# Splitting a weight load unevenly over the two halves of the partitions, in a decode kernel with attention and an MLP

## The chip, the cores and the metric

The kernel runs on one core of a Trainium2 chip. The metric is the device time of one execution in microseconds (us), as the median of several runs. One further execution was taken with the hardware profiler; the profile that is quoted comes from it.

## The reference

One decode step for a batch of two tokens. The input is normalized once and goes both to an attention block over a long cache and to a two-layer MLP; both results are added to the input.

```python
def _A_ref(x, k_cache, v_cache, wq, wo):          # x: 2 x 1 x 512
    B, Sq, D = x.shape
    H, Dh = 32, 128                                # caches: 2 x 32 x 8192 x 128, bf16
    q = (x @ wq).reshape(B, Sq, H, Dh).transpose(0, 2, 1, 3)
    scores = jnp.einsum("bhqd,bhkd->bhqk", q, k_cache) * (Dh ** -0.5)
    p = _softmax(scores, axis=-1)
    o = jnp.einsum("bhqk,bhkd->bhqd", p, v_cache)
    return o.transpose(0, 2, 1, 3).reshape(B, Sq, H * Dh) @ wo

def _B_ref(x, w1, w2):                             # w1: 512 x 1792, w2: 1792 x 512
    h = jnp.maximum(jnp.einsum("bsd,df->bsf", x, w1), 0)
    return jnp.einsum("bsf,fd->bsd", h, w2)

xn = _layernorm(x)                                 # x = A_x; B_x is not used
return x + _A_ref(xn, K, V, wq, wo) + _B_ref(xn, w1, w2)
```

K and V together are 268 MB, the weights 12 MB. All arrays are bf16.

## The kernel before

The kernel writes its five instruction streams out by hand: SP issues loads, PE does matmuls and transposes, DVE (vector) and ACT (scalar) empty PSUM, POOL prepares constants and small copies. Semaphores tie them together; there is no scheduler that reorders anything.

**Loads.** All large loads go through SP's queue in the order in which they are written (L163 to L187): wq into the second V buffer, w1, w2, then K0, K1, V0. The 64 heads (2 tokens x 32) are taken two at a time, as 32 pairs; the K of a pair is one load of 4 MB (`load_k`, L158), and so is its V (`load_v`, L161): 128 partitions with 32 KB each. There are two K buffers and two V buffers. The next K load is issued when PE has done the last group of transposes of the pair that holds the buffer (`pT[NG - 1]`), the next V load when PE has finished the weighted sum of the pair that holds its buffer (`sW`). At the end the last V comes in two halves and wo in five pieces of 14, 7, 6, 3 and 2 rows a partition (`cuts`). The small load of x goes by ACT's queue (L164).

**The opening.** DVE and ACT compute the layer norm; PE transposes xn (L234) and multiplies it with wq (L240, 32 matmuls), then with w1 (L253, 56 matmuls), whose result `hp` lies transposed in PSUM: hidden unit f on a partition. Of w2 each partition p holds the 14 consecutive rows 14p to 14p+13 (L170), and w1's columns are read with a stride of 14 to match. DVE takes the relu of `hp` into `hT` (L446). PE waits for `hT` and for w2 (`dW2`) and runs 14 matmuls of 128 x 2 by 128 x 512 into `y` (L270). DVE adds x and leaves the sum in `ys` (L456). Only then does PE begin the loop over the pairs.

**The loop.** For a pair, PE transposes K in 16 groups of eight 128 x 128 blocks (L285), DVE and ACT copy each group to SBUF (L412), and PE multiplies it with q (L292). The weighted sum of V (L305) is that of the pair before, whose softmax is already done. The order on PE is fixed in `step`.

**The closing.** PE sums the softmax denominators (L360) and puts `ys` transposed into the PSUM tile `fin` with four fp32 matmuls against a 2 x 2 identity (L363), with `start` on the first; then the weighted sum of the last V, small transposes and selections (L378, L383), and the 128 matmuls with wo (L397), which accumulate onto `fin` piece by piece as `dW` allows. DVE casts `fin` to `yT` (L502), PE transposes it (L406), DVE copies it out (L504), and SP stores it (L189).

Of the kernel before, what the change touches and what calls it, by code (L numbers as in the profile page):

```python
# [7 lines left out]
ALU = mybir.AluOpType  # L8
# [11 lines left out]
def kernel(  # L20
# [13 lines left out]
    P = 128  # L34
    HP = P // 2
    bf16 = mybir.dt.bfloat16
    f32 = mybir.dt.float32

    Bsz, Sq, D = A_x.shape
    _, H, Sk, Dh = A_k_cache.shape  # L40
    Dff = B_w1.shape[1]
    assert Dh == P and D % P == 0 and Dff % P == 0 and Sk % HP == 0
    KT = D // P
    FT = Dff // P
# [3 lines left out]
    WJ = H * Dh // P  # L48
# [4 lines left out]
    QG = H * Dh // 512  # L53
    QH = 512 // Dh
    Z = (QG - 1) * Bsz
    inv_sqrt = float(Dh) ** -0.5
    eps = 1e-5

# [2 lines left out]
    def sb(shape, dt, name):  # L61
        return ctx.enter_context(nc.sbuf_tensor(name, shape, dt))
# [4 lines left out]
    def sem(name):  # L67
        return tc.alloc_semaphore(name)
# [2 lines left out]
    ks = [sb([P, SLOT], bf16, f"ks{i}") for i in range(R)]  # L71
    vs = [sb([P, SLOT], bf16, f"vs{i}") for i in range(R)]

    w_sb = sb([P, max(WJ * D, KT * Dff + FT * D)], bf16, "w_sb")
    w1_sb = w_sb[:, 0:KT * Dff].rearrange("p (kt f) -> p kt f", kt=KT)
    w2_sb = w_sb[:, KT * Dff:KT * Dff + FT * D].rearrange("p (j n) -> p j n", j=FT)
    wo_sb = w_sb[:, 0:WJ * D].rearrange("p (j n) -> p j n", j=WJ)
    kT = [sb([P, EG, P], bf16, f"kT{i}") for i in range(4)]
    identb = sb([P, P], bf16, "identb")
# [24 lines left out]
    OTn = sb([P, Bsz, H], bf16, "OTn")  # L104
    Ob = sb([H, Bsz, Dh], bf16, "Ob")
    OX = sb([P, WJ, Bsz], bf16, "OX")
    hT = sb([P, FT, Bsz], bf16, "hT")
    ys = sb([Bsz, D], f32, "ys")
    yT = sb([P, Bsz, KT], bf16, "yT")
    osb = sb([Bsz * KT, P], bf16, "osb")  # L110

# [11 lines left out]
        return Sc[i][:, 480:482]  # L123


    dX, dO, dW1, dW2 = sem("dX"), sem("dO"), sem("dW1"), sem("dW2")
    dK = [sem(f"dK{i}") for i in range(R)]
    dV = [sem(f"dV{i}") for i in range(R)]
    dH = [sem(f"dH{i}") for i in range(2)]
# [21 lines left out]
    )  # L151
    hp = ot[1][:, 0:FT * Bsz].rearrange("p (j b) -> p j b", b=Bsz)
    y = Sc[1][0:Bsz, :]
    fin = ot[0][:, 0:KT * Bsz].rearrange("p (b c) -> p c b", c=KT)


# [10 lines left out]
    @(lambda f: f(nc.sync))  # L167
    def _(sp):
        sp.dma_start(w1_sb, B_w1.rearrange("(p kt) f -> p kt f", kt=KT)).then_inc(dW1, 16)  # L169
        sp.dma_start(w2_sb, B_w2.rearrange("(p j) n -> p j n", j=FT)).then_inc(dW2, 16)  # L170
        load_k(0)
        load_k(1)
        load_v(0)
        for t in range(NP - 2):
            sp.wait_ge(pT[NG - 1], t + 1)
            load_k(t + R)
            sp.wait_ge(sW, t + 1)
            load_v(t + 1)
        sp.wait_ge(sW, NP - 1)
        for i in range(2):  # L180
            sl = slice(i * SLOT // 2, (i + 1) * SLOT // 2)
            sp.dma_start(  # L182
                vs[(NP - 1) % R][:, sl], V_all[(NP - 1) * P:NP * P, sl]
            ).then_inc(dH[i], 16)
        for c in range(NC):
            sl = slice(cuts[c], cuts[c + 1])
            sp.dma_start(wo_sb[:, sl, :], wo_v[:, sl, :]).then_inc(dW[c], 16)  # L187
        sp.wait_ge(sE, 1)
        sp.dma_start(  # L189
            out.rearrange("b s (c p) -> (b s c) p", p=P), osb[:]  # L190
        ).then_inc(dO, 16)
# [38 lines left out]
    def _(pe):  # L230
# [16 lines left out]
        i.then_inc(sQ, 1)  # L247
        pe.wait_ge(dW1, 16)

        w1_v = w1_sb.rearrange("p kt (f j) -> p kt j f", j=FT)  # L250
        for j in range(FT):
            for kt in range(KT):
                i = pe.matmul(  # L253
                    hp[:, j, :],
                    lhsT=w1_v[:, kt, j, :],
                    rhs=xz[:, kt, Z:Z + Bsz],
                    start=(kt == 0),
                    stop=(kt == KT - 1),
                )
# [6 lines left out]
        i.then_inc(sQ, 1)  # L266
        pe.wait_ge(sF, 2)
        pe.wait_ge(dW2, 16)
        for j in range(FT):
            i = pe.matmul(  # L270
                y,
                lhsT=hT[:, j, :],
                rhs=w2_sb[:, j, :],
                start=(j == 0),
                stop=(j == FT - 1),
            )
        i.then_inc(sF, 1)

# [81 lines left out]
            t = pe.matmul(dbp[:, :, u], lhsT=onesh[:, u, :], rhs=RS[:], start=True, stop=True)  # L360
        t.then_inc(sH, 1)
        for k in range(KT):
            pe.matmul(  # L363
                fin[:, k, :],
                lhsT=ys[:, k * P:(k + 1) * P],
                rhs=ident2[:],
                start=(k == 0),
                stop=False,
            )
        for i in range(2):  # L370
            pe.wait_ge(dH[i], 16)
            for e in range(i * NG // 2, (i + 1) * NG // 2):
# [9 lines left out]
        for dq in range(DQ):  # L382
# [4 lines left out]
                start=(dq == 0),  # L387
# [5 lines left out]
        for c in range(NC):  # L393
            pe.wait_ge(dW[c], 16)
            for j in range(cuts[c], cuts[c + 1]):
                for k in range(KT):
                    t = pe.matmul(  # L397
                        fin[:, k, :],
                        lhsT=wo_sb[:, j, k * P:(k + 1) * P],
                        rhs=OX[:, j, :],  # L400
                        start=False,
                        stop=(j == WJ - 1 and k == KT - 1),
                    )
        t.then_inc(sH, 1)
# [10 lines left out]
    @(lambda f: f(nc.vector))  # L415
    def _(v):
        v.memset(eps_t[:], eps).then_inc(sV, 1)
        v.memset(onesb[:], 1.0)
        v.memset(xz[:], 0.0).then_inc(sZ, 1)
        v.memset(prm[R - 1][:], 0.0).then_inc(sP, 1)  # L420
        v.wait_ge(dX, 16)
        v.bn_stats(out=stats[:], in_=xsb[:]).then_inc(sV, 1)
        v.wait_ge(sV, 2)
        v.bn_aggr(out=mv[:], in_=stats[:]).then_inc(sV, 1)
        v.wait_ge(sA, 1)
        v.reciprocal(out=rinv[:], in_=rstd[:]).then_inc(sV, 1)
        v.wait_ge(sV, 4)

        v.tensor_scalar(
            out=xn[:],  # L430
            in0=xsb[:].rearrange("b (p kt) -> b kt p", kt=KT),
            scalar1=mv[:, 0:1],
            scalar2=rinv[:, 0:1],
            op0=ALU.subtract,
            op1=ALU.mult,
        ).then_inc(sV, 1)
        v.wait_ge(sQ, 1)
        v.wait_ge(sZ, 1)
        v.tensor_copy(xz[:, :, Z:Z + Bsz], tpx).then_inc(sV, 1)
        v.wait_ge(sQ, 2)  # L440

        v.tensor_scalar(  # L442
            out=qs[:], in0=qp, scalar1=inv_sqrt, scalar2=None, op0=ALU.mult
        ).then_inc(sV, 1)
        v.wait_ge(sF, 1)
        v.tensor_scalar(  # L446
            out=hT[:], in0=hp, scalar1=0.0, scalar2=None, op0=ALU.max,
        ).then_inc(sF, 1)
        v.wait_ge(sQ, 3)

        v.tensor_copy(
            qb[:].rearrange("p (b g l) -> p l g b", b=Bsz, l=QH),
            tpq.rearrange("p l (g b) -> p l g b", b=Bsz),
        ).then_inc(sV, 93)
        v.wait_ge(sF, 3)
        v.tensor_tensor(out=ys[:], in0=y, in1=xsb[:], op=ALU.add).then_inc(sF, 1)  # L456

        def pair(i, n):
            for e in range(NG):
                if e not in ON_ACT:  # L460
                    v.wait_ge(pT[e], n)
                    kcopy(v, e)
            v.wait_ge(sS, n)
            for u in range(2):
                half = slice(u * HP, (u + 1) * HP)
                m = v.tensor_reduce(  # L466
                    out=mcol[i][half, :], in_=S_of(i)[half, :, u], axis=AX.X, op=ALU.max
                )
            m.then_inc(sM, 1)
            v.wait_ge(sT, n)  # L470
            v.tensor_reduce(  # L471
                out=mx[i][:], in_=tr_of(i).rearrange("o (u m) -> o u m", u=2),
                axis=AX.X, op=ALU.max, negate=True,
            ).then_inc(sX, 1)

        reg = nc.alloc_register(mybir.EngineType.DVE, "pairno_v")
        v.reg_mov(reg, 0)
        with v.Fori(0, NP // R):
            for r in range(R):
                v.reg_add(reg, reg, 1)  # L480
                pair(r, reg)

        v.wait_ge(sH, 1)
        v.reciprocal(out=RD[:], in_=Sc[0][:, 0:N]).then_inc(sV, 1)
        v.wait_ge(sV, 101)
        v.wait_ge(sO, NP + 1)
        on = OTn[:].rearrange("p b h -> p (b h)")
        v.tensor_tensor(
            out=on[:, 0:N - 2], in0=OTf[:, 2:N], in1=RD[:, 0:N - 2], op=ALU.mult
        ).then_inc(sV, 1)  # L490
        v.wait_ge(sW, NP + 1)
        v.tensor_tensor(
            out=on[:, N - 2:N], in0=ot[1][:, 0:2], in1=RD[:, N - 2:N], op=ALU.mult
        ).then_inc(sV, 1)
        v.wait_ge(sH, 2)
        v.tensor_copy(Ob[:], tp[0][0:H, 0:Bsz, :]).then_inc(sV, 1)
        v.wait_ge(sH, 3)
        v.tensor_copy(
            OX[:], Sc[1][:, 0:Bsz * WJ].rearrange("p (b j) -> p j b", b=Bsz)
        ).then_inc(sV, 1)  # L500
        v.wait_ge(sH, 4)
        v.tensor_copy(yT[:], ot[0][:, 0:KT * Bsz].rearrange("p (b c) -> p b c", c=KT)).then_inc(sV, 1)  # L502
        v.wait_ge(sH, 5)
        v.tensor_copy(osb[:], tp[1][0:Bsz * KT, 0, :]).then_inc(sE, 1)  # L504


    @(lambda f: f(nc.scalar))
    def _(a):
        a.wait_ge(sV, 3)
        a.activation(  # L510
            out=rstd[:], in_=mv[:, 1:2], func=ACTF.Sqrt, bias=eps_t[:Bsz], scale=1.0
        ).then_inc(sA, 1)


        def out_copy(r, n, c):
# [59 lines left out]
```

## Time and profile before

| | |
|---|---|
| median of 3 runs | 660.92 us (660.83 to 660.98) |
| profiled execution: time, span | 660.69 us, 658.6 us |
| busy share PE, weight loads, DVE, ACT, POOL | 85%, 81%, 38%, 39%, 1% |
| moved by DMA | 280.66 MB, 426 GB/s over the span |
| granted TensorE clock, mean | 0.944 |
| median from issue to landing, K load and V load | 26.7 us, 31.3 us |

A busy share is an average over the whole span; of several engines with high shares, the one that sets the time is found by asking what each waits for. PE's share includes modelled ends of pipelined matmuls. A queue's line in the profile gives packets (one for each row of a load and one for each engine's semaphore write), megabytes, and the time of its packets as a share of the sixteen DMA engines' span. In the timeline, a line gives start, duration, engine, line of the kernel and what is written and read; in brackets stands the idle time ahead of it and what ended it. The chain of work that ended last is put down to DMA for 58% and to PE for 37%.

### The profile page before, as it was taken

The numbers are of one execution on the slowest core, as the hardware profiler recorded it, in microseconds if no ns is written. First come the engines' busy times: TensorE is split into PE (matmuls) and PEld (weight loads), VectorE is DVE, ScalarE is ACT, GpSimd is POOL, SyncE is SP. The second block draws the span as 40 slices with busy tenths as digits, with TensorE's granted clock in tenths as the row PEclk, the third lists the DMA queues.
The fourth block names the chain that finished last, engine by engine and source line by source line (L and its number), as shares of the span: only waits on it lengthen the run. The fifth ranks groups of instructions, "written<-read, shape, count | busy, mean of one in ns | idle before, by whom it ended". The sixth has DMA issues, their size and how long they took to land.

```text
span 658.6 us, 26859 instructions
## 1 busy us (share of the span) xinstructions
PE 559.9 (85%) x12737; PEld 535.1 (81%) x12737; DVE 253.2 (38%) x436; ACT 255.8 (39%) x403; POOL 9.0 (1%) x46
## 2 busy tenths in 40 slices
PE   2998799987989878879887887997878997887896
PEld 0488798987879878879887887987878987887895
DVE  1144344442434433334443343443434443333441
ACT  1043444443433434334353434344333444333340
POOL 1000000000000000000000000000000000000000
PEclk9799999998998988999898899898989998898988
DMA  8999999999999999999999999999999999999996
GB/s 365 430 444 418 439 430 429 432 428 442 422 442 424 436 428 432 432 428 444 420 442 428 432 430 430 434 430 442 424 436 428 432 432 428 440 424 442 426 424 281
DMA packets 10542, 280.66 MB, mean 426 GB/s; under 512 B 1186, under 2 KB 1188, under 8 KB 1700
## 3 DMA queue, kind: packets, MB, share of 16 engines
q1 hardware_dynamic: 10528, 280.50, 99.2%
q8 instruction: 9, 0.15, 0.1%
q14 instruction: 1, 0.01, 0.0%
q10 hardware_dynamic: 4, 0.00, 0.0%
HBM read 280.50 MB, written 0.00 MB: 426 GB/s over the span
## 4 chain that ended last, share of the span: by engine, by line
DMA 58%; PE 37%; ACT 2%; issue 1%; SPq 1%; ACTq 0%; DVE 0%
DMA ks<-in_A_k_cache_dram 54%; PE tp L285 21%; PE Sc L292 11%; PE ot L305 4%; DMA w_sb<-in_A_wo_dram 4%; ACT kT L412 2%; ACT L412 1%; SPq L187 0%; PE Sc L340 0%; SPq L182 0%; PE Sc L343 0%; SPq L170 0%; SPq L169 0%; SPq L163 0%; PE ot L397 0%
## 5 line engine op out<-in xcount | busy, mean ns | idle before, releaser
L285 PE MATMUL tp<-identb,ks 128*128 128x128 bf16 x4096 | 323.5, 229 | 68.4 <-DMA ks<-in_A_k_cache_dram 68.4
L412 DVE COPY kT<-tp 128x1024 bf16<-128x1024 bf16 x320 | 219.7, 691 | 324.3 <-PE tp L285 324.2
L285 PEld LDWEIGHTS tp<-identb,ks 128*128 128x128 bf16 x4096 | 254.8, 102 | 72.3 <-DMA ks<-in_A_k_cache_dram 72.2
L412 ACT COPY kT<-tp 128x1024 bf16<-128x1024 bf16 x192 | 194.3, 1012 | 233.4 <-PE tp L285 233.3
L292 PE MATMUL Sc<-q,kT 128*128 128x64 bf16 x4096 | 216.8, 196 | 7.6 <-ACT kT L412 5.7
L292 PEld LDWEIGHTS Sc<-q,kT 128*128 128x128 bf16 x4096 | 178.4, 100 | 11.3 <-ACT kT L412 9.0
L305 PE MATMUL ot<-prm,vs 128*128 128x64 bf16 x4224 | 156.1, 192 | 4.2 <-issue 4.2
L305 PEld LDWEIGHTS ot<-prm,vs 128*128 128x128 bf16 x4224 | 139.0, 97 | 7.0 <-issue 4.4
L525 ACT COPY nm<-Sc 128x2 f32<-128x2 f32 x32 | 5.1, 160 | 118.5 <-PE Sc L343 118.5
L529 ACT ACTIVATE prm<-Sc,nm 64x128 bf16<-64x128 f32 x64 | 25.7, 401 | 4.3
L466 DVE TENSOR_REDUCE mcol<-Sc 64x1 bf16<-64x128 f32 x64 | 18.6, 290 | 18.7 <-PE Sc L292 18.3
L412 ACT ACT_TABLE_LOAD x16 | 20.5, 1283 | 2.2
L240 PE MATMUL ot<-vs,xz 128*16 128x512 bf16 x32 | 9.5, 470 | 8.6 <-DMA vs<-in_A_wq_dram 8.6
L517 ACT COPY OTf<-ot 128x2 f32 x32 | 5.1, 160 | 26.9 <-PE ot L305 26.9
L471 DVE TENSOR_REDUCE mx<-Sc 1x2 bf16<-1x128 bf16 x32 | 8.9, 278 | 16.9 <-PE Sc L340 16.9
L240 PEld LDWEIGHTS ot<-vs,xz 128*16 128x16 bf16 x32 | 3.3, 105 | 14.4 <-issue 12.2
L225 POOL COPY q<-qb 128x2 bf16<-128x2 bf16 x32 | 5.8, 184 | 588.9 <-PE Sc L292 566.1
L529 ACT ACTIVATION_READ_ACCUMULATOR prm<-Sc,nm x64 | 11.8, 185 | 0.0
L442 DVE TENSOR_SCALAR qs<-ot 16x512 bf16<-16x512 f32 x1 | 0.7, 679 | 18.0 <-PE ot L240 18.0
L340 PE MATMUL Sc<-identb,mcol 128*1 128x128 bf16 x32 | 7.0, 217 | 0.0
L270 PE MATMUL Sc<-w_sb,hT 128*2 128x512 bf16 x14 | 5.8, 604 | 0.1
L343 PE MATMUL Sc<-mx,onesb 1*128 1x2 bf16 x32 | 5.5, 172 | 0.0
(56 smaller groups left out, 37.5 us busy)
## 6 DMA issues: line engine op xcount, KB each, us to landing
ks<-in_A_k_cache_dram SPq DMA_DIRECT2D x32, 4096.0 KB, 26.7
vs<-in_A_v_cache_dram SPq DMA_DIRECT2D x31, 4096.0 KB, 31.3
vs<-in_A_wq_dram SPq DMA_DIRECT2D x1, 4096.0 KB, 12.1
vs<-in_A_v_cache_dram SPq DMA_DIRECT2D x2, 2048.0 KB, 19.3
w_sb<-in_B_w_dram SPq DMA_DIRECT2D x2, 1792.0 KB, 17.9
w_sb<-in_A_wo_dram SPq DMA_DIRECT2D x1, 1792.0 KB, 25.4
w_sb<-in_A_wo_dram SPq DMA_DIRECT2D x1, 896.0 KB, 27.1
w_sb<-in_A_wo_dram SPq DMA_DIRECT2D x1, 768.0 KB, 28.5
```

The lines of the kernel that those rows point to most:

```text
L225: g.tensor_copy(q2[t % R][:], qb[:, 2 * t:2 * t + 2]).then_inc(sQ1, 1)
L240: i = pe.matmul(qp, lhsT=xz[:, kt, Z - g * Bsz:Z - g * Bsz + QG * Bsz], rhs=vs[1][:, (kt * QG + g) * 512:(kt * QG + g + 1) * 512], start=( ...
L270: i = pe.matmul(y, lhsT=hT[:, j, :], rhs=w2_sb[:, j, :], start=(j == 0), stop=(j == FT - 1),)
L285: t = pe.transpose(tp[e % 4][:, i, :], ks[r][:, kk * Dh:(kk + 1) * Dh], identb[:])
L292: t = pe.matmul(Sc[r][:, 2 * kk:2 * kk + 2 * REP], lhsT=kT[e % 4][:, i, :], rhs=rep(q2[r][:]), start=True, stop=True,)
L305: t = pe.matmul(ot[r][:, 0:2 * REP], lhsT=vs[r][:, kk * Dh:(kk + 1) * Dh], rhs=rep(prm[r][:, kk, :]), start=(kk == 0), stop=(kk == KB - 1),)
L340: pe.transpose(tr_of(r), mcol[r][:], identb[:]).then_inc(sT, 1)
L343: pe.matmul(bc_of(r), lhsT=onesb[:], rhs=mx[r][:], start=True, stop=True).then_inc(sB, 1)
L412: fn(kT[e % 4][:], tp[e % 4][:]).then_inc(kR[e], 1)
L466: m = v.tensor_reduce(out=mcol[i][half, :], in_=S_of(i)[half, :, u], axis=AX.X, op=ALU.max)
L471: v.tensor_reduce(out=mx[i][:], in_=tr_of(i).rearrange("o (u m) -> o u m", u=2), axis=AX.X, op=ALU.max, negate=True,).then_inc(sX, 1)
L529: x = a.activation(out=prm[i][half, :, u], in_=S_of(i)[half, :, u], func=ACTF.Exp, bias=nm[i][half, u:u + 1], scale=1.0, accum_out=RS[half ...
```

## The change

The last 256 rows of w2 no longer lie on all 128 partitions. Every partition gets 12 consecutive rows of the first 1536 by SP's queue (`FA`), and the 256 rows that are left go to the lower 64 partitions alone, four to each (`FB`), so that the lower ones hold 16 and the upper ones 12. Those four rows come by ACT's queue, in eight loads of 8 partitions each: partitions p, p+4, ..., p+28, for p of 0 to 3 and 32 to 35, with four separate rows of 1 KB for each partition. They are issued by ACT after the square root of the layer norm and count on a semaphore of their own, `dW2b`.

What has to follow: w1's columns are read with a stride of 12 for the first 12 groups and without one for the last two; the relu becomes three instructions, of which two split the last two groups of `hp` into lower and upper halves and put both on the lower 64 partitions; PE waits for `dW2b` too, and runs 16 matmuls instead of 14, the last four on 64 partitions. The tile `w_sb` keeps its size, which wo sets.

Beside this, the closing takes `ys` in another way: PE transposes it into a corner of the PSUM bank of `fin`, DVE copies that to `xT`, the wo products start `fin` themselves, and the last cast becomes an addition of `xT`.

```diff
+    FA = FT - 2
+    FB = 2 * (FT - FA)
+    FJ = FA + FB
...
-    w2_sb = w_sb[:, KT * Dff:KT * Dff + FT * D].rearrange("p (j n) -> p j n", j=FT)
+    w2_sb = w_sb[:, KT * Dff:KT * Dff + FJ * D].rearrange("p (j n) -> p j n", j=FJ)
...
-        sp.dma_start(w2_sb, B_w2.rearrange("(p j) n -> p j n", j=FT)).then_inc(dW2, 16)
+        sp.dma_start(
+            w2_sb[:, 0:FA, :], B_w2[0:P * FA, :].rearrange("(p j) n -> p j n", j=FA)
+        ).then_inc(dW2, 16)
...
-        w1_v = w1_sb.rearrange("p kt (f j) -> p kt j f", j=FT)
+        w1_a = w1_sb[:, :, 0:P * FA].rearrange("p kt (f j) -> p kt j f", j=FA)
...
-                    lhsT=w1_v[:, kt, j, :],
+                    lhsT=w1_a[:, kt, j, :] if j < FA else w1_sb[:, kt, j * P:(j + 1) * P],
...
         pe.wait_ge(dW2, 16)
-        for j in range(FT):
+        pe.wait_ge(dW2b, 16 * 8)
+        for j in range(FJ):
+            half = slice(0, HP if j >= FA else P)
             i = pe.matmul(
                 y,
-                lhsT=hT[:, j, :],
-                rhs=w2_sb[:, j, :],
+                lhsT=hT[half, j, :],
+                rhs=w2_sb[half, j, :],
...
         for k in range(KT):
-            pe.matmul(
-                fin[:, k, :],
-                lhsT=ys[:, k * P:(k + 1) * P],
-                rhs=ident2[:],
-                start=(k == 0),
-                stop=False,
-            )
+            t = pe.transpose(yst[:, k, :], ys[:, k * P:(k + 1) * P], ident2[:])
+        t.then_inc(sH, 1)
...
-                        start=False,
+                        start=(j == 0 and k == 0),
...
-        v.tensor_scalar(
-            out=hT[:], in0=hp, scalar1=0.0, scalar2=None, op0=ALU.max,
-        ).then_inc(sF, 1)
+        for o, h in (
+            (hT[:, 0:FA, :], hp[:, 0:FA, :]),
+            (hT[0:HP, FA:FJ:2, :], hp[0:HP, FA:FT, :]),
+            (hT[0:HP, FA + 1:FJ:2, :], hp[HP:P, FA:FT, :]),
+        ):
+            t = v.tensor_scalar(out=o, in0=h, scalar1=0.0, scalar2=None, op0=ALU.max)
+        t.then_inc(sF, 1)
...
+        v.wait_ge(sH, 2)
+        v.tensor_copy(xT[:], yst)
...
-        v.tensor_copy(yT[:], ot[0][:, 0:KT * Bsz].rearrange("p (b c) -> p b c", c=KT)).then_inc(sV, 1)
+        v.tensor_tensor(
+            out=yT[:],
+            in0=ot[0][:, 0:KT * Bsz].rearrange("p (b c) -> p b c", c=KT),
+            in1=xT[:].rearrange("p c b -> p b c"),
+            op=ALU.add,
+        ).then_inc(sV, 1)
...
+        w2_v = B_w2[P * FA:, :].rearrange("(j p) n -> p j n", p=HP)
+        for p in (0, 1, 2, 3, 32, 33, 34, 35):
+            sl = slice(p, p + 29, 4)
+            a.dma_start(w2_sb[sl, FA:FJ, :], w2_v[sl]).then_inc(dW2b, 16)
```

More of the change, by code (lines that the diff above doesn't have):

```diff
@@ L72 @@
     vs = [sb([P, SLOT], bf16, f"vs{i}") for i in range(R)]
-    w_sb = sb([P, max(WJ * D, KT * Dff + FT * D)], bf16, "w_sb")
+    w_sb = sb([P, max(WJ * D, KT * Dff + FJ * D)], bf16, "w_sb")
     w1_sb = w_sb[:, 0:KT * Dff].rearrange("p (kt f) -> p kt f", kt=KT)
-    w2_sb = w_sb[:, KT * Dff:KT * Dff + FT * D].rearrange("p (j n) -> p j n", j=FT)
+    w2_sb = w_sb[:, KT * Dff:KT * Dff + FJ * D].rearrange("p (j n) -> p j n", j=FJ)
     wo_sb = w_sb[:, 0:WJ * D].rearrange("p (j n) -> p j n", j=WJ)
@@ L106 @@
     OX = sb([P, WJ, Bsz], bf16, "OX")
-    hT = sb([P, FT, Bsz], bf16, "hT")
+    hT = sb([P, FJ, Bsz], bf16, "hT")
     ys = sb([Bsz, D], f32, "ys")
+    xT = sb([P, KT, Bsz], f32, "xT")
     yT = sb([P, Bsz, KT], bf16, "yT")
@@ L123, in bc_of @@
         return Sc[i][:, 480:482]
-    dX, dO, dW1, dW2 = sem("dX"), sem("dO"), sem("dW1"), sem("dW2")
+    dX, dO, dW1 = sem("dX"), sem("dO"), sem("dW1")
+    dW2, dW2b = sem("dW2"), sem("dW2b")
     dK = [sem(f"dK{i}") for i in range(R)]
@@ L153 @@
     y = Sc[1][0:Bsz, :]
+    yst = ot[0][:, 16:16 + KT * Bsz].rearrange("p (c b) -> p c b", c=KT)
     fin = ot[0][:, 0:KT * Bsz].rearrange("p (b c) -> p c b", c=KT)
@@ L268, in _ @@
         pe.wait_ge(dW2, 16)
-        for j in range(FT):
+        pe.wait_ge(dW2b, 16 * 8)
+        for j in range(FJ):
+            half = slice(0, HP if j >= FA else P)
             i = pe.matmul(
                 y,
-                lhsT=hT[:, j, :],
-                rhs=w2_sb[:, j, :],
+                lhsT=hT[half, j, :],
+                rhs=w2_sb[half, j, :],
                 start=(j == 0),
-                stop=(j == FT - 1),
+                stop=(j == FJ - 1),
             )
@@ L494, in _ @@
         ).then_inc(sV, 1)
-        v.wait_ge(sH, 2)
+        v.wait_ge(sH, 3)
         v.tensor_copy(Ob[:], tp[0][0:H, 0:Bsz, :]).then_inc(sV, 1)
-        v.wait_ge(sH, 3)
+        v.wait_ge(sH, 4)
         v.tensor_copy(
@@ L500, in _ @@
         ).then_inc(sV, 1)
-        v.wait_ge(sH, 4)
-        v.tensor_copy(yT[:], ot[0][:, 0:KT * Bsz].rearrange("p (b c) -> p b c", c=KT)).then_inc(sV, 1)
         v.wait_ge(sH, 5)
+        v.tensor_tensor(
[4 more added lines that the diff above has]
+        ).then_inc(sV, 1)
+        v.wait_ge(sH, 6)
         v.tensor_copy(osb[:], tp[1][0:Bsz * KT, 0, :]).then_inc(sE, 1)
```

## The prediction

> **What bounds the kernel now.** I read the page first, then the waits of the DMA queue, then the timeline of the first 90 us and of the last 20, and last the trace's own records of packets and of semaphore landings, which give each DMA row's start and duration and, for each load, the sixteen times at which its engines finished.
>
> The page's list of DMA queues:
>
> ```profile
> DMA packets 10542, 280.66 MB, mean 426 GB/s; under 512 B 1186, under 2 KB 1188, under 8 KB 1700
> q1 hardware_dynamic: 10528, 280.50, 99.2%
> q8 instruction: 9, 0.15, 0.1%
> ```
>
> SP's queue (q1) fills the sixteen DMA engines for 99.2% of the span. So the time is the bytes of the slowest engine, so long as SP always has a load queued. Whether it has is seen in the waits of SP's queue (waited for: us in total, times, longest) and in its issues (start, us):
>
> ```profile
> SPq L158 <- PE tp L285: 429.8, 30, 39.8
> SPq L161 <- PE ot L305: 148.6, 30, 8.2
> ```
>
> ```profile
> 43.72 0.33 SPq L158 DMA_DIRECT2D ks<-in_A_k_cache_dram  x1
> ...
> 83.61 0.33 SPq L158 DMA_DIRECT2D ks<-in_A_k_cache_dram  x1
> ```
>
> Each K load waits for PE's transposes to free its buffer. The first load's rows start 1.04 us after its issue (0.96 to 2.00), so K2, issued at 43.72, could start at 44.8, while V0 ahead of it occupies its engines to 50.2 (landing 50.67 on most, and a row ends 0.43 before it is seen to land: 32.30 against 32.73 for K0). Spare: 5.5 us. For K4, issued at 83.61, V2 runs to 89.2: spare 4.5 us, the least of all. These spares decide below.
>
> PE's side, from the timeline:
>
> ```profile
> 26.50 5.84 PE L270 MATMUL Sc<-w_sb,hT 128*2 128x512 bf16 x14
> ...
> 32.77 1.51 PE L285 MATMUL tp<-identb,ks 128*128 128x128 bf16 x24 [0.43 <-DMA ks<-in_A_k_cache_dram]
> ...
> 654.90 0.37 PE L397 MATMUL ot<-OX,w_sb 128*128 128x2 bf16 x8 [0.16 <-DMA w_sb<-in_A_wo_dram]
> ```
>
> The w2 product (0.417 us a matmul) ends just before pair 0 begins. The end is set by the last wo piece: it lands at 654.85 and 3.7 us follow.
>
> The landing records show what the page doesn't: that last piece reached half of its engines at 653.04 to 653.44 and the other half at 654.67 to 654.85. The gap grew engine by engine: one engine falls 1.3 us behind at K0, seven are behind by 109 us, the eighth from 651. Each step follows one of the nine 16 KB instruction packets of q8 (29.6, 41.8, 47.8, 55.0, 61.1, 68.3, 107.2, 650.4, 654.3). Such a packet takes 1.06 us, fifteen data rows run beside it instead of sixteen, and the next row on its engine takes 1.7 us instead of 1.22. Eight late engines of sixteen: which? The x load of two rows ran just before wq; two engines land 0.1 us after their group from then on, and they are never among the late eight.
>
> [...]no view names engines, so the late half being the upper one is likely, not shown. [...]the fetch at 29.57 went between two rows of K0's load.[...]
>
> **The change part by part.**
>
> *Bytes.* The w2 load on SP's queue falls from 14,336 to 12,288 bytes a partition. A 14,336-byte packet took 0.5365 us; by the slope to 7,168 (0.2754) 12,288 costs 0.462. Eight on each engine: −0.6 us on all. [...]x's 1 KB took 0.044, 2 KB took 0.085, so 0.046 each, plus eight semaphore writes of 0.009: +1.54, net +0.94 us. Upper half: 654.85 − 0.6 = 654.25; lower: 653.44 + 0.94 = 654.38. The end would move by −0.47 us if nothing else happened.
>
> *ACT.* Eight issues after rstd (ends 3.49), at the 0.56 us of the x issue: to 8 us. ACT's next work for others is the copy of pair 0 at 33.4; the table load of 1.28 us between hides too. Cost nothing.
>
> *Matmuls and hT.* Two more w2 matmuls: 16 × 0.417 = 6.67 us, +0.83. The relu becomes three DVE instructions (0.19 once now; two small ones add about 0.3 with their gaps). Both delay pair 0 by about 1.1 us, less than the 4.5 us of spare: nothing by themselves. qb behind them comes 0.3 later, under the w2 product.
>
> *Tail.* Four transposes replace the four fp32 matmuls of L363 (1.05 us), with 8 columns' copy (about 0.17) on DVE; PE's V products follow at 644.6 and have slack to the wo pieces. From below: the matmuls' whole 1.05, hidden; from above the same again, hidden up to the 0.2 us by which PE waits for the 653.29 piece. The final add against the copy of 0.17: a tensor_tensor took 0.16 at 2 columns and 0.22 at 62, so +0 to 0.05 on the path.
>
> *The wait dW2b.* PE waits for all eight small loads ahead of its first w2 matmul; behind it stand pair 0's transposes, and behind these K2's issue. The rows first reach the engines at 3.49 + 0.95 (the x load's 0.92 to 1.87) = 4.4, when the third wq row (1.22 us each) is running. If ACT's queue gets one 1 KB row for each row of SP's, the 32 rows pair off with wq rows 3 to 8 (6), w1's 8, w2's 8, K0's 8 and two of K1's. K0 lands at 31.2 on an undisturbed engine; two rows (2.4) and the added 1.0 of bytes give 34.6. PE then starts pair 0 at 34.6 + 6.8 = 41.4 instead of 32.77: 8.6 us late. It catches up (pairs take it 16 to 17 us from the third on, a K and V load 19.4), but not in time: K2 and K4 come late, and the queue stands empty for 8.6 − 4.5 = 4.1 us by K4. That idle time levels the early lags, but the engine hit at 650.4 is still late at the end, so the balance brings nothing. The profiled execution took 660.69 (span 658.6): 664.8; the median is 0.2 higher, so **665.0**.
>
> How sure is 34.6? If semaphore writes also take turns, on both queues, 40 entries against nine a load end at K1's sixth row: 39.5, 13.5 us late, +9.0. If only SP's take turns, 31.0: +0.5 to 1. So this case spans 661.5 to 670.
>
> **The rivals.**
>
> *In time.* A load's four rows go as one packet, or ACT's rows are served faster than SP's: eight turns end inside wq, before 15 us, PE waits for nothing new, and only bytes count: −0.47 + 0.05, **660.5**. It ends on the other side; it decides from the point where the small loads land before about 30 us (start 4 us late, within the spare). For it: the 4.4 us arrival against a need at 27. Against: the fetch shows turns row by row for 32 KB rows. By this mechanism the gain can't exceed half the gap, 0.65 us, which is 0.1%.
>
> *A price for each turn.* The only change of queue in the trace is the instruction fetch: 1.33 us for 16 KB whose bytes are worth 0.62, so 0.71 is lost. If each of 32 turns costs that, 23 us more: the rows land at 57 and the end is 27 us later, **687**; with eight turns, 5.7 us on the lower half: 653.44 + 0.94 + 5.7, **666**. For it: the row after each fetch takes 0.46 longer. Against: [...]two filled queues may overlap.
>
> *The wrong half.* If the late engines were the lower ones, the bytes load them: +0.94, **661.9**.
>
> **How the numbers follow.** A measurement of this kernel tells about 0.2% (1.3 us) from no change. Turns row by row with PE waiting: 0.45 (0.40 slower, 0.05 within). In time: 0.30 (0.28 within, 0.02 faster). A price for each turn: 0.16, slower. The wrong half: 0.05, within. Something else: 0.04, half faster, half slower. Sum: faster 0.04, within 0.38, slower 0.58. The range, 660.2 to 671.5, holds the second case and nearly all of the first; most of the third is left out. The first case's own range is 661.5 to 670.
>
> **What would show it.** The 1 KB packets of ACT's queue spread from 4.4 to about 34 us (in time: all before 15; priced turns: each SP row between them 1.7 us). PE's wait ahead of the w2 matmuls put down to a w_sb load, ending at 31 to 40. Pair 0's transposes at 41. An empty stretch in the DMA rates near 50 us. In time instead: pair 0 at about 34, no new wait, and the last piece's sixteen landings within 0.5 us. The forecast is wrong if pair 0 starts before 37 or the DMA share stays at 99%.

## The result: 671.22 us, slower by 1.5%

The changed kernel takes 671.22 us in the median of six runs (669.76 to 671.87), the kernel before 660.95 (660.64 to 661.28). The ratio is 1.0153, 95% interval 1.014 to 1.0166. The profiled execution took 671.38 us with a span of 669.3, 10.7 above the span of before.

The forecast was 665.0 with a range of 660.2 to 671.5: the way and the mechanism hold, but the change measured, 10.3 us, is two and a half times the 4.1 that were forecast.

The page's list of DMA queues, changed kernel:

```profile
DMA packets 10863, 280.67 MB, mean 419 GB/s; under 512 B 1250, under 2 KB 1508, under 8 KB 2020
...
q1 hardware_dynamic: 10528, 280.24, 97.6%
q10 hardware_dynamic: 324, 0.26, 0.1%
```

SP's queue no longer fills the engines: 97.6% of the span against 99.2%. ACT's queue (q10) holds 324 packets: 256 rows of 1 KB and 64 semaphore writes from the small loads, and four packets from the x load. Where SP's queue stands empty is seen in the busy share of the DMA engines, in tenths, for forty equal slices of the span (the kernel before, then the changed one):

```profile
DMA  8999999999999999999999999999999999999996
...
DMA  8994999999999999999999999999999999999996
```

and closer in the busy time by stage (stage, its length, busy time of each engine, granted clock, DMA share, GB/s):

```profile
core 0: us, PE busy (x) PEld busy (x) DVE busy (x) ACT busy (x) POOL busy (x), PEclk, DMA share, GB/s
0.00:48.00 48.00, 19.65 (x113) 8.57 (x114) 3.65 (x14) 3.05 (x4) 3.44 (x16) 0.79 0.97 409
48.00:60.00 12.00, 11.79 (x275) 11.62 (x275) 7.50 (x11) 6.07 (x6) 0.00 (x0) 1.00 0.25 93
60.00:667.00 607.00, 527.84 (x12355) 514.16 (x12351) 242.38 (x414) 246.85 (x393) 5.60 (x30) 0.94 1.00 428
```

Between 48 and 60 us the DMA share is 0.25; before and after it is whole. The quarter is nearly all the end of V0; 9 us are lost in one place, while PE is at its busiest. The timeline shows who is late:

```profile
3.21 5.82 ACTq L535 DMA_DIRECT2D w_sb<-in_B_w_dram  x8
...
41.94 6.09 PE L281 MATMUL Sc<-w_sb,hT 128*2 128x512 bf16 x16 [15.09 <-DMA w_sb<-in_B_w_dram]
47.97 1.51 PE L296 MATMUL tp<-identb,ks 128*128 128x128 bf16 x24
...
58.91 0.33 SPq L165 DMA_DIRECT2D ks<-in_A_k_cache_dram  x1
```

PE waits 15.09 us for a load into w_sb, begins pair 0 at 47.97 instead of 32.77 (15.2 us late), and K2 is issued 15.2 us late, at 58.91 instead of 43.72. V0, the last load in the queue, had left its engines between 49.7 and 51.2.

The packet records show the small rows themselves. They don't name engines, but an engine's packets follow each other end to start and can be chained. Each small load writes its semaphore on eight engines (64 writes for eight loads), by the chains on the same eight each time. The forecast calls these eight the lower ones and the other eight the upper, and so does what follows; which partitions an engine writes no view shows. On each of the eight engines that carry small rows, one entry of ACT's queue (a 1 KB row of 0.046 us, or a semaphore write of 0.009) follows one entry of SP's queue; this pair is called a turn below. So the four rows of a partition are four turns, which the prediction had left open. The first rows run at 7.66 us, and the eight loads end, counted by their semaphore writes, at about 12.7, 15.0, 17.3, 19.8, 22.5, 28.8, 33.8 and 40.1 (two engines one turn later, at 41.1 and 41.3). The last landing is at 41.81.

### The profile page after: what moved, and what is told of

It reads as the page before. It is cut to its first block, busy times and chain, and to the rows that moved or that the text cites. A ratio compares the mean times of both kernels' runs of the same rounds, so it can differ in the third digit from the quotient of the medians.

```text
span 669.3 us, 26866 instructions
## 1 busy us (share of the span) xinstructions
PE 559.3 (84%) x12735; PEld 534.4 (80%) x12735; DVE 253.5 (38%) x439; ACT 256.0 (38%) x403; POOL 9.0 (1%) x46
## 3 DMA queue, kind: packets, MB, share of 16 engines
q1 hardware_dynamic: 10528, 280.24, 97.6%
## 4 chain that ended last, share of the span: by engine, by line
DMA 58%; PE 37%; ACT 2%; issue 1%; ACTq 1%; SPq 0%; DVE 0%
DMA ks<-in_A_k_cache_dram 48%; PE tp L296 21%; PE Sc L303 11%; DMA w_sb<-in_B_w_dram 5%; DMA w_sb<-in_A_wo_dram 4%; PE ot L316 4%; ACT kT L418 2%; PE Sc L281 1%; ACTq L535 1%; ACT L418 1%; SPq L196 0%; DMA xsb<-in_A_x_dram 0%; PE Sc L351 0%; SPq L191 0%; PE Sc L354 0%
## 5 line engine op out<-in xcount | busy, mean ns | idle before, releaser
L281 PE MATMUL Sc<-w_sb,hT 128*2 128x512 bf16 (+1 forms) x16 | 6.1, 557 | 15.1 <-DMA w_sb<-in_B_w_dram 15.1
L281 PEld LDWEIGHTS Sc<-w_sb,hT 128*2 128x2 bf16 (+1 forms) x16 | 1.6, 110 | 19.1 <-issue 18.9
```

The lines of the kernel that those rows point to most:

```text
L281: i = pe.matmul(y, lhsT=hT[half, j, :], rhs=w2_sb[half, j, :], start=(j == 0), stop=(j == FJ - 1),)
```

## The experiments

Seven kernels, told in the order of what they settle. "Theory" in the quoted expectations is what was held before each ran.

**Same rows, no turns.** The eight small loads go by SP's queue, behind its w2 load.

```diff
         ).then_inc(dW2, 16)
+        w2_v = B_w2[P * FA:, :].rearrange("(j p) n -> p j n", p=HP)
+        for p in (0, 1, 2, 3, 32, 33, 34, 35):
+            sl = slice(p, p + 29, 4)
+            sp.dma_start(w2_sb[sl, FA:FJ, :], w2_v[sl]).then_inc(dW2b, 16)
         load_k(0)
...
-            a.dma_start(w2_sb[sl, FA:FJ, :], w2_v[sl]).then_inc(dW2b, 16)
```

> The changed kernel with the eight small w2 loads issued by SP right behind its w2 load, instead of by ACT. Nothing takes turns. Theory (the loss is the late landing of rows that take turns one by one on ACT's queue): the small rows land at about 22.5, PE does not wait for them, pair 0 starts at about 34.5, the DMA share is back at 99%, and only the bytes count: 660.4 to 660.6 us, with the last wo piece landing on all sixteen engines within 0.5 us, because the late half is the upper one. Rival (the split itself, the 64-partition matmuls, the relu in three parts or the closing cost the time): 668 to 672. Rival (the late engines are the lower half): 661.9, with the last landings 2.8 us apart.

Measured: 661.55 us against 660.87, ratio 1.0011 (1.0003 to 1.002). The timeline:

```profile
2.35 5.85 SPq L183 DMA_DIRECT2D w_sb<-in_B_w_dram  x8
...
26.39 6.23 PE L285 MATMUL Sc<-w_sb,hT 128*2 128x512 bf16 x16 [0.31 <-DVE hT L461]
...
32.55 1.51 PE L300 MATMUL tp<-identb,ks 128*128 128x128 bf16 x24
```

The small rows land at 22.9, PE waits for hT alone, pair 0 starts at 32.55, and nearly all of the loss is gone. So the split, the 64-partition matmuls, the relu in three parts and the closing are not what costs 10 us. But the forecast gain of 0.3 to 0.5 us is not there either: the time is 0.7 us above the kernel before, and the last wo piece reaches the sixteen engines 3.0 us apart instead of within 0.5. By these two numbers the last rival (661.9 and 2.8 us apart) comes closer than the theory; the groups of landings further below show how far it holds.

**Same queue, fewer entries.** The four rows of a partition are consecutive, so each 8-row load has eight rows of 4 KB.

```diff
-        w2_v = B_w2[P * FA:, :].rearrange("(j p) n -> p j n", p=HP)
+        w2_v = B_w2[P * FA:, :].rearrange("(p j) n -> p j n", p=HP)
...
+        w1_b = w1_sb[:, :, P * FA:].rearrange("p kt (f j) -> p kt j f", j=FB)
-        for j in range(FT):
+        for j in range(FJ):
             for kt in range(KT):
                 i = pe.matmul(
-                    hp[:, j, :],
-                    lhsT=w1_a[:, kt, j, :] if j < FA else w1_sb[:, kt, j * P:(j + 1) * P],
+                    hp[0:HP if j >= FA else P, j, :],
+                    lhsT=w1_a[:, kt, j, :] if j < FA else w1_b[:, kt, j - FA, :],
...
-            (hT[0:HP, FA:FJ:2, :], hp[0:HP, FA:FT, :]),
-            (hT[0:HP, FA + 1:FJ:2, :], hp[HP:P, FA:FT, :]),
+            (hT[0:HP, FA:FJ, :], hp[0:HP, FA:FJ, :]),
```

> The changed kernel with the last 256 rows of w2 dealt out so that the four rows of a partition are consecutive: each of the eight loads on ACT's queue has one row of 4 KB for each partition instead of four of 1 KB (w1's last columns read with a stride of 4, four products of 64 columns instead of two of 128). Same bytes, same queue, same loads; entries per engine fall from 40 to 16. Theory (one entry a turn, semaphore writes counted): from 7.7 us on 5 turns in wq, 9 in w1, 2 in w2: all landed by 19, PE does not wait, 660.4 to 660.7 us. Rival (turns cost by bytes or by load, or ACT's queue is slow whatever the entries): still landing at 35 to 41, 666 to 671.

Measured: 661.28 us against 660.87, ratio 1.0005 (0.9997 to 1.0013).

```profile
3.63 5.36 ACTq L535 DMA_DIRECT2D w_sb<-in_B_w_dram  x8
...
27.11 5.39 PE L282 MATMUL Sc<-w_sb,hT 128*2 128x512 bf16 x16 [0.15 <-DVE hT L457]
```

ACT issues at nearly the same pace, the first row runs at 7.65, the bytes are the same; what differs on the queue is that they come in fewer and longer entries. All has landed by 19.73 instead of 41.81, and PE waits for hT alone. The wait is set by entries, one a turn, not by bytes and not by ACT's queue as such. The time itself was forecast at 660.4 to 660.7; again the gain is missing, though the 0.4 us above the kernel before lie within the interval.

**The wait without the change.** The kernel before, with one line ahead of its w2 product:

```diff
         pe.wait_ge(dW2, 16)
+        pe.wait_ge(dK[1], 16)
```

> The kernel before with one more wait: PE waits for K1's landing (42.45 us in the profile) ahead of its w2 product. No split, no load on ACT's queue. Theory: the product runs 42.5 to 48.3, pair 0 starts 15.6 us late, K2 and K4 are issued late, SP's queue stands empty, and the end moves by 15.6 less K4's spare of 4.5: +11.1, 672.0 us, with an empty stretch at 51 to 60. Rival (the small loads cost the DMA engines time by themselves): clearly less, 665 or under.

Measured: 670.69 us against 660.87, ratio 1.0147 (1.0132 to 1.0163). Timeline, and the DMA row of the slices:

```profile
42.67 5.04 PE L271 MATMUL Sc<-w_sb,hT 128*2 128x512 bf16 x14 [15.72 <-DMA ks<-in_A_k_cache_dram]
47.65 1.51 PE L286 MATMUL tp<-identb,ks 128*128 128x128 bf16 x24
```

```profile
DMA  8994999999999999999999999999999999999996
```

Pair 0 starts 14.9 us late, the same fourth slice of 16.7 us is more than half empty as in the changed kernel, and the time is the changed kernel's but for half a microsecond. The late start of PE alone is enough for the whole loss; taking turns costs the DMA engines nothing that shows. The forecast of 672.0 was 1.3 too high: the w2 product took 5.04 us, not 5.8, and the spare that it subtracts is not the one that counted (see the part on the spare below).

**A smaller dose.** The same with K0's landing.

```diff
         pe.wait_ge(dW2, 16)
+        pe.wait_ge(dK[0], 16)
```

> The kernel before with one more wait: PE waits for K0's landing (32.73 us) ahead of its w2 product: pair 0 starts at about 38.7, 6.0 us late. Theory (a late start costs only what exceeds the least spare of SP's queue, K4's 4.5 us): +1.4, 662.3 us. Rival (a late start is paid in full): 667. Rival (all of it is caught up): 660.9.

Measured: 662.08 us against 660.87, ratio 1.0019 (1.0008 to 1.0029); its runs lie apart, 661.1 to 663.54.

```profile
38.75 1.51 PE L286 MATMUL tp<-identb,ks 128*128 128x128 bf16 x24
...
49.69 0.33 SPq L158 DMA_DIRECT2D ks<-in_A_k_cache_dram  x1
...
70.31 0.33 SPq L158 DMA_DIRECT2D ks<-in_A_k_cache_dram  x1
```

Six microseconds late cost 1.2 in the median. Lateness is paid only above a spare, as forecast; of the rivals, payment in full is ruled out. That the number fits (662.3 forecast) is in part luck: the profile, which is of the slowest of the eight executions, shows the engines partly idle from 50 to 52 and from 70 to 74, ahead of K2 and of K3, and not ahead of K4, whose spare the forecast subtracted. Why K3 came late there, and why the executions differ by 2.4 us, stays open.

**An earlier issue.** The changed kernel, with ACT's eight issues moved ahead of its wait for the statistics.

```diff
+        w2_v = B_w2[P * FA:, :].rearrange("(j p) n -> p j n", p=HP)
+        for p in (0, 1, 2, 3, 32, 33, 34, 35):
+            sl = slice(p, p + 29, 4)
+            a.dma_start(w2_sb[sl, FA:FJ, :], w2_v[sl]).then_inc(dW2b, 16)
         a.wait_ge(sV, 3)
...
-            a.dma_start(w2_sb[sl, FA:FJ, :], w2_v[sl]).then_inc(dW2b, 16)
```

> The changed kernel with the eight small loads issued by ACT at once after the x load, ahead of the wait for the statistics (1.5 us instead of 3.2). Theory (40 entries, one a turn, against the rows of SP's queue): the issue is 1.7 us earlier, so one or two more wq rows are paired off and the last row comes one or two K1 rows sooner: landing at 38.5 to 40.5, 669.0 to 670.5 us. Rival (ACT's late first row, 7.66, is what makes it late): the first row at about 2.5 and all landed before 30: 661 to 662.

Measured: 669.29 us against 660.9, ratio 1.0122 (1.0107 to 1.0138).

```profile
1.52 5.81 ACTq L529 DMA_DIRECT2D w_sb<-in_B_w_dram  x8
...
39.73 6.56 PE L281 MATMUL Sc<-w_sb,hT 128*2 128x512 bf16 x16 [13.32 <-DMA w_sb<-in_B_w_dram]
```

The first small row runs at 6.46 instead of 7.66, one wq row earlier, and the last lands at 39.59, in the forecast range. PE's product starts 2.2 us earlier: one turn of 1.2 us is the earlier first row, and the other is that here no engine is a turn behind. The count of turns is the cause, the start only shifts it.

**The closing alone.** The kernel before with the transposes, the copy and the addition of the changed closing.

```diff
-            pe.matmul(
-                fin[:, k, :],
-                lhsT=ys[:, k * P:(k + 1) * P],
-                rhs=ident2[:],
-                start=(k == 0),
-                stop=False,
-            )
+            t = pe.transpose(yst[:, k, :], ys[:, k * P:(k + 1) * P], ident2[:])
+        t.then_inc(sH, 1)
...
-                        start=False,
+                        start=(j == 0 and k == 0),
...
+        v.wait_ge(sH, 2)
+        v.tensor_copy(xT[:], yst)
...
-        v.tensor_copy(yT[:], ot[0][:, 0:KT * Bsz].rearrange("p (b c) -> p b c", c=KT)).then_inc(sV, 1)
...
+        v.tensor_tensor(
+            out=yT[:],
+            in0=ot[0][:, 0:KT * Bsz].rearrange("p (b c) -> p b c", c=KT),
+            in1=xT[:].rearrange("p c b -> p b c"),
+            op=ALU.add,
+        ).then_inc(sV, 1)
```

> The kernel before with the closing of the changed one alone: ys transposed into PSUM, copied to xT, added at the last cast. No split of w2. Theory (costs nothing): 660.8 to 661.0 us. Rival (the closing is the reason why the two versions without the late wait, small loads on SP's queue and one 4 KB row, stand 0.4 to 0.7 us above the kernel before): 661.3 to 661.6.

Measured: 660.89 us against 660.9, ratio 0.9999 (0.9991 to 1.0008). It costs nothing; the 0.4 to 0.7 us of the two versions above come from elsewhere.

**Which engines are late.** Where the gain went is read from the last landings of the two versions without the late wait. The last wo piece reaches the sixteen engines in three groups. With the small loads on SP's queue: two engines at 652.71 and 652.86, twelve at 653.88 to 654.60, two at 655.65 and 655.70. With 4 KB rows: two at 652.42 and 652.64, twelve at 653.73 to 654.38, two at 655.30 and 655.41. By the split the upper eight, which carry no small rows, are about 1.5 us ahead of the lower eight, as K0's landings show with the small loads on SP's queue (seven engines at 30.41 to 30.88, the eighth, hit by then, among the nine at 31.93 to 32.30), and an instruction fetch puts an engine 1.3 us back (in the kernel before, K0 lands on fifteen engines at 31.01 to 31.39, and at 32.73 on the one hit by the fetch at 29.57). So the twelve are the six upper engines that were hit with the six lower ones that were not, the first two are upper engines not hit, the last two lower ones that were. Followed load by load, the hits of both versions fall in the same order: three upper (five upper engines are left in front at V0), two lower (two engines stand alone at the end at K2), three upper (two are left in front at the end). The last two, which now carry the extra rows, end 0.85 and 0.56 us after the 654.85 of before; the times rose by 0.68 and 0.41, and only the first rise is clear of no change by its interval.

To see the same in the kernel before, marks were put on its engines:

```diff
...
+        mark_v = A_wo.rearrange("(p j) n -> p (j n)", j=16)
+        sl = slice(0, 29, 4)
+        sp.dma_start(mark[sl, :], mark_v[sl, :]).then_inc(dM, 16)
+        for p in (1, 2, 3):
+            sl = slice(p, p + 13, 4)
+            sp.dma_start(mark[sl, :], mark_v[sl, :]).then_inc(dM, 16)
+        for p in (32, 33, 34):
+            sl = slice(p, p + 5, 4)
+            sp.dma_start(mark[sl, :], mark_v[sl, :]).then_inc(dM, 16)
         load_k(0)
...
+        sp.wait_ge(dM, 16 * 7)
         sp.wait_ge(sE, 1)
```

> The kernel before with seven more loads on SP's queue behind w2, of 16 KB rows into a tile that nothing reads: one load of 8 partitions, three of 4, three of 2. [...]The marks stay apart through the whole run, so each engine that an instruction fetch delays by 1.3 us is seen to leave its own group. Theory A (the late eight are the upper half): all eight steps are seen in the unmarked group of eight. Theory B, after the 4 KB version and the one on SP's queue (six of the late are upper, two are lower): six steps in the unmarked group, two in the marked ones[...]. [...]about 663.8 us.

Measured: 663.57 us, a single run. K0 lands in four groups: seven unmarked engines at 31.02 to 31.40 and one at 32.69, hit by the fetch at 28.3; four at 31.67 to 31.79; two at 33.71 and 34.00; two at 35.51 and 35.56. At 0.615 us for a row of 16 KB, as the last V halves took in the kernel before, the distances are those of one, four and seven marks: the smaller loads fell on engines that the larger had used. The four engines with four and seven marks keep their distance to the last V half and beyond, so none of them is ever hit, and the first two hits are on unmarked engines. After that the run decides nothing: PE began pair 0 at 35.61, K2 was issued at 47.77, and the idle time levelled the unmarked engines with the four of one mark. That two lower engines are hit in the kernel before as well, and that they are among the four of one mark, is carried over from the two versions above and not shown by itself; nor is it shown that the unmarked engines are the upper eight.

## Why the prediction was right and wrong, point by point

**What bounds the kernel: right.** With SP's queue full the time follows the slowest engine (in the two versions without the late wait its last landing came 0.85 and 0.56 us later, the end 0.68 and 0.41); the whole loss is the one empty stretch and the restart behind it.

**The deciding mechanism: right.** One row a turn, PE held at dW2b, K2 late, the queue empty near 50 us. Each of the four marks named for it is in the profile, but later than named: the rows spread from 7.66 to 40 (4.4 to 34 forecast), PE's wait is put down to the w_sb load and ends at 41.94 (31 to 40), pair 0 starts at 47.97 (41), and the stretch lies at 51 to 59 (near 50). The 4 KB rows and the wait on K1 show its two halves apart: entries make the rows late, and the late PE makes the time.

**The landing of the small rows: mis-sized, 34.6 forecast, 41.81 measured.** This is the term that failed; it made pair 0 late by 15.2 us, not 8.6. The forecast took the rows alone as turns. Semaphore writes take turns on both queues: behind the 40 entries of ACT's queue on an engine (32 rows, 8 semaphore writes) stand four wq rows and the semaphore write, nine entries each of w1, w2 and K0, and eight of K1, the last of them behind the last semaphore write. The alternative that the forecast worked out for this, 39.5, was near. The rest: the first small row came behind the fourth wq row, not the third (1.2 us), and two of the eight engines were one turn further behind. The reading "4.4, when the third wq row is running" was itself off: in the profile of before all sixteen engines run their second row at 4.4, because the first row of each takes 1.91 us in the mean. And the small rows came not at 4.4 but at 7.66, after three of SP's rows had started since ACT's issue.

**The spare: the wrong load, and a term left out.** The forecast subtracted K4's 4.5 us. PE made up time sooner than taken: in the changed kernel K4 is issued 11.0 us later than before, no longer 15.2,

```profile
94.64 0.33 SPq L165 DMA_DIRECT2D ks<-in_A_k_cache_dram  x1
```

and V2, issued at 82.64 and landed from 99.75 on, still covers it. K2's spare of 5.5 decided. Left out was the restart of an empty queue: the sixteen first rows of K2 take 1.99 us in the mean against 1.21. The first rows of wq, on engines just as idle, show nearly the same in the profile of before (the 1.91 above), so the term could have been read there. So the estimate becomes 15.2 − 5.5 + 0.8 = 10.5, against 10.7 in the spans; the forecast's 8.6 − 4.5 = 4.1 had too small a lateness and too small a spare. The wait on K1 fits the same sum, with first rows of K2 of 1.89 us there: 14.9 − 5.5 + 0.7 = 10.1, against 10.2 in the spans.

**The bytes: sizes right, the premise wrong.** A 12,288-byte packet took 0.460 (forecast 0.462), a 1 KB row 0.046. But the late engines are not the upper half: the text called that likely, not shown (it was the author's assumption), and the landings of the two versions without the wait show six upper and two lower. In the changed kernel itself the empty stretch levels the halves, as forecast: K2 lands on fifteen engines at 70.62 to 71.28, and at the end five engines are late by about 1.3 us (664.91 to 665.53, the others 663.46 to 664.12), as many as there are fetches from 66.5 to 660.3. That the x load's two engines are never among the late eight told only that these two were not hit. So the rival in time, which gave 660.5, would have given 661.3 to 661.6 once PE doesn't wait, and the rival of the wrong half was a quarter right: two of eight.

**A price for each turn: refuted.** SP's rows between the small ones take their usual 1.213 us in the median, 0.460 in w2 and 0.535 in w1. The dear change of queue in the profile of before, 0.71 us lost, was measured at an instruction fetch; the small rows show no such loss.

**Costed at nothing: right** for the closing (0.9999 alone). The relu and the two matmuls are in the version with the small loads on SP's queue, and pair 0 starts at 32.55 there, not later than the 32.77 of before. ACT's issues were longer than taken, 5.82 us for eight, still hidden.

No version here beats the kernel before. What the split could still bring is, as an estimate from the gap of 1.3 us between the early and the late eight engines, at most half of it, 0.65 us or 0.1%, and would need rows aimed at single engines.

## What to carry to other kernels

When two queues feed the same DMA engines, count entries, not bytes: each 1 KB row, and each semaphore write, waited here for one entry of the other queue, mostly a whole row of 12 to 32 KB, so 32 KB an engine took 33 us to arrive; rows of 4 KB or a place in the same queue took that away. Before putting a new load ahead of an engine's long stretch of work, follow whose buffers that engine frees and how long the queue can run without it; only lateness above that spare is paid, and then about one to one (here 6.0 us late cost 1.2, 14.9 late cost 9.8), and a queue that has run empty pays for its restart (1.99 us for K2's first rows here, against 1.21). An imbalance should be seen by engine before it is corrected by halves.

## What the runs showed of the hardware that was not expected

- A semaphore write takes a turn of its own between the queues, like a data row: 40 turns for 32 rows. The last four small loads' first semaphore writes run at 22.52, 28.77, 33.82 and 40.08: 6.25 us apart where five rows of K0 or K1 lie between (five at 1.213 and 0.046 make 6.3), 5.05 where one of the five entries is K0's semaphore write.
- ACT's first small row ran 4.45 us after its issue began, at 7.66, and 4.94 us after it at 6.46 when issued at 1.52; the x load on idle engines took 0.94. In both cases three of SP's rows started on an engine between the issue and its first small row (four on two engines of the first case).
- An issue of an 8-row load with four rows a partition takes 0.73 us of ACT's or SP's queue (5.82 and 5.85 for eight), with one row a partition 0.67 (5.36 for eight), a 128-row load 0.33 to 0.42.
- The first row on each of sixteen idle engines takes 1.99 us in the mean (K2 behind the empty stretch) and 1.91 (wq, before), against 1.21 for a row of the same 32 KB in a full queue.
- The instruction fetches hit the same sequence of halves in the two versions where it could be followed (three upper, two lower, three upper), each costing its engine about 1.3 us, as K0's landing at 32.73 against 31.39 in the kernel before.
